# Two-layer network behind clustered attention, one core: the first pair of heads ranks raw centroid products, and the other preparation moves by an iteration

## The chip, the cores and the metric

The program runs on one core of one Trainium2 chip. The metric is device time in microseconds (us), the median of repeated executions of the whole program; lower is better. Engines are named as the profile names them: PE is TensorE (PEld its weight loads), DVE is VectorE, ACT is ScalarE, POOL is GpSimd and SP is SyncE, which here only issues DMA transfers.

## What is computed

Attention within clusters, then two feed-forward layers. The first pair of heads, which the change is about, goes through the cluster assignment like every other.

```python
def _attn_ref(q, k, v, centroids):            # batch 2, heads 8, seq 768, head_dim 64, 16 clusters
    q_n = q / (np.linalg.norm(q, axis=-1, keepdims=True) + 1e-06)
    k_n = k / (np.linalg.norm(k, axis=-1, keepdims=True) + 1e-06)
    c_n = centroids / (np.linalg.norm(centroids, axis=-1, keepdims=True) + 1e-06)
    q_assign = np.argmax(np.einsum('bhsd,hcd->bhsc', q_n, c_n), axis=-1)
    k_assign = np.argmax(np.einsum('bhsd,hcd->bhsc', k_n, c_n), axis=-1)
    mask = q_assign[:, :, :, None] == k_assign[:, :, None, :]
    scores = np.where(mask, scale * np.matmul(q, k.transpose(0, 1, 3, 2)), -1000000000.0)
    ... softmax(scores) @ v

x = attn_out                                   # 1536 tokens x 512
x = leaky_relu(x @ w_in) @ w_out               # d_ff 2048
h = x @ moe2_w_in
out = (P(h) / (Q(h) + 1e-06)) @ moe2_w_out     # cubic over quadratic in |h|
```

## The kernel before

The 16 heads are worked in eight pairs. A head has six query tiles of 128 rows, so a pair is twelve units and the attention 96. A hand-written loop `run` goes over iterations i. Iteration i takes the row maximum of unit i on VectorE (`nm`, L592), divides two units by their sums on GpSimd when i is even (`e`, L619, of units i-2 and i-1), transposes the probabilities of unit i-4 on TensorE (`pT`, L627), takes the exponential of unit i on ScalarE (`e`, L603), and forms the scores of unit i+1 on TensorE (`s`, L583, first with `a`, then with `b`). The transposed probabilities are split in a rounded part `ph` (ScalarE, L640) and a rest `pl` (VectorE, L646), and multiplied with the values `vs`.

Each pair p has to be prepared before its units come up. The rows of q and k are loaded (`qraw`, `kraw`), transposed (`pa`, L243), copied by ScalarE (`x`, L246), and multiplied with the centroids on TensorE (`sims`, L326); the products are copied to `sv` (L337). VectorE then takes the maximum over the 16 clusters (`mx`), marks where it is reached, numbers the marks (`rank`, L362), takes the first (L365) and compares again for the one-hot rows (`oh`). These go through TensorE, ScalarE (`ot`, L429) and six DMA transfers (L436) into the lower rows of `b`, where they mask the scores. The high and low parts of q and k (`hl`, L293 and L298 on GpSimd) go to `a` and `b` by DMA (L305: four transfers for `a`, two for `b` per head). The values `v` of a pair are loaded into one buffer, `vraw` (L233), and split by GpSimd, once per head of the pair (`vsplit`, L447 and L448).

Which iteration does which piece is a table for each pair: an entry (-9, "end", rank) of pair p puts it at the end of iteration 12p-9; "act", "pe", "pa" and "dve" are places earlier in the iteration. Each engine works through its own instructions in the order in which the program issues them, and waits for what it needs; SyncE's transfers stand in one queue in the same way. All GpSimd work and all `vsplit` calls are thus in one order with the divisions `e`.

Pair 0 and the first head of pair 1 are prepared in `startup`, written out by hand ahead of the loop. There the centroids are normalised first, by twelve small VectorE operations (L116 to L129), then transposed into `cc`, and only then multiplied. The first head's one-hot rows go into `b` without DMA (`on`, L387; `po`, L401; L409 and L411), its `a` and `b` parts too (`direct_hi` on ScalarE, `direct_lo` on VectorE L281, `direct_b` on GpSimd L286). The multiplications `warm` (L722) on constant data compute nothing that is used; they keep TensorE occupied.

Of the kernel before, what the change touches and what calls it, by code (L numbers as in the profile page):

```python
# [9 lines left out]
F32 = mybir.dt.float32  # L10
# [8 lines left out]
P = 128  # L19
# [11 lines left out]
def clustered_attention_moe_moe2(  # L31
# [81 lines left out]
    def exact_norm_ops(y, r, ss):  # L113
        vec = nc.vector
        return [
            lambda: vec.tensor_scalar(  # L116
                y.bitcast(I32), ss.bitcast(I32), 0.5, SQRT_MAGIC, op0=ALU.mult, op1=ALU.add
            ),
            lambda: vec.reciprocal(r, y),
            lambda: vec.tensor_tensor(r, r, ss, op=ALU.mult),  # L120
            lambda: vec.tensor_tensor(y, y, r, op=ALU.add),
            lambda: vec.reciprocal(r, y),
            lambda: vec.scalar_tensor_tensor(r, r, 2.0, ss, op0=ALU.mult, op1=ALU.mult),
            lambda: vec.scalar_tensor_tensor(y, y, 0.5, r, op0=ALU.mult, op1=ALU.add),
            lambda: vec.reciprocal(r, y),
            lambda: vec.scalar_tensor_tensor(r, r, 2.0, ss, op0=ALU.mult, op1=ALU.mult),
            lambda: vec.scalar_tensor_tensor(y, y, 0.5, r, op0=ALU.mult, op1=ALU.add),
            lambda: vec.tensor_scalar(y, y, 0.5, 1e-6, op0=ALU.mult, op1=ALU.add),
            lambda: vec.reciprocal(r, y),  # L129
        ]  # L130
# [11 lines left out]
    class Attention:  # L142
# [27 lines left out]
        def load_centroids(self):  # L170
            self.tok.tile([P, 104], F32, name="fill", bufs=1)
            self.ct = self.tok.tile([P, D], F32, name="ct", bufs=1)
            nc.scalar.dma_start(out=self.ct, in_=cent.rearrange("h c d -> (h c) d"))
            nc.scalar.preload_act_table_set("natural_log_exp_and_others")

        def centroid_ops(self):
            sm = self.tok
            ct = self.ct
            sq = sm.tile([P, D], F32, name="csq", bufs=1)
            ss = sm.tile([P, 1], F32, name="css", bufs=1)  # L180
            y = sm.tile([P, 1], F32, name="cy", bufs=1)
            r = sm.tile([P, 1], F32, name="cr", bufs=1)
            ch = sm.tile([P, 2, D], F32, name="ch", bufs=1)
            self.ch = ch
            vec = nc.vector
            ops = [
                lambda: vec.tensor_tensor(sq, ct, ct, op=ALU.mult),
                lambda: vec.reduce_sum(ss, sq, axis=AX.X),
            ]
            ops += exact_norm_ops(y, r, ss)  # L190
            return ops + [
                lambda a=a: vec.tensor_scalar(ch[:, a], ct, r, None, op0=ALU.mult)
                for a in range(2)
            ]
# [1135 lines left out]
```

## Time and profile before

| | before |
|---|---|
| median of 3 runs | 791.07 us (790.88 to 791.53) |
| the profiled execution | 791.8 us |
| span of its records, first to last instruction | 789.7 us |
| TensorE busy | 776.2 us, 98% |
| VectorE, ScalarE, GpSimd busy | 645.8, 510.6, 387.9 us |
| mean granted TensorE clock | 0.997 of 2.4 GHz |
| attention: until about | 262 us |
| feed-forward layers | from 262 us on |

The span is what the trace shows; the profiled execution took 2.1 us more than it. A busy share is an average over the whole program. What a stage is worth is read from the stretch in question: which engine has no idle time there, and what the others wait for. Times in the rows below count from the first instruction.

### The profile page before, as it was taken

The numbers are of one execution on the slowest core, as the hardware profiler recorded it, in microseconds if no ns is written. First come the engines' busy times: TensorE is split into PE (matmuls) and PEld (weight loads), VectorE is DVE, ScalarE is ACT, GpSimd is POOL, SyncE is SP. The second block draws the span as 40 slices with busy tenths as digits, with TensorE's granted clock in tenths as the row PEclk, the third lists the DMA queues.
The fourth block names the chain that finished last, engine by engine and source line by source line (L and its number), as shares of the span: only waits on it lengthen the run. The fifth ranks groups of instructions, "written<-read, shape, count | busy, mean of one in ns | idle before, by whom it ended". The sixth has DMA issues, their size and how long they took to land.

```text
span 789.7 us, 11946 instructions
## 1 busy us (share of the span) xinstructions
PE 776.2 (98%) x4026; PEld 660.1 (84%) x4026; DVE 645.8 (82%) x1106; ACT 510.6 (65%) x1015; POOL 387.9 (49%) x400
## 2 busy tenths in 40 slices
PE   8899999999998999999999999999999999999997
PEld 6699999899887888888888888888888888888886
DVE  7888999998998678877577568759988888888896
ACT  5789998998899455454254246357766666666662
POOL 3876987877567324230041023267645545553341
PEclk9999999999999999999999999999999999999999
DMA  3686663662320334345445353530101001000012
GB/s 103 158 210 140 154 150 83 150 159 78 93 91 1 107 107 161 106 142 205 134 156 181 128 175 114 180 106 30 52 13 41 27 27 41 15 0 1 1 54 107
DMA packets 42109, 78.58 MB, mean 100 GB/s; under 512 B 5248, under 2 KB 25280, under 8 KB 42048
## 3 DMA queue, kind: packets, MB, share of 16 engines
q1 hardware_dynamic: 41760, 77.65, 33.3%
q8 instruction: 32, 0.52, 0.3%
q14 instruction: 29, 0.24, 0.1%
q10 hardware_dynamic: 288, 0.16, 0.1%
HBM read 49.84 MB, written 9.96 MB: 76 GB/s over the span
## 4 chain that ended last, share of the span: by engine, by line
PE 87%; DVE 6%; ACT 3%; POOL 1%; issue 1%; DMA 0%; DVEq 0%; ACTq 0%; POOLq 0%
PE h L1097 33%; PE y L1097 31%; PE o L663 7%; PE s L583 6%; PE pT L627 6%; PE sims L326 3%; DVE pl L646 2%; DVE nm L592 2%; PE pa L243 1%; ACT ph L640 1%; ACT e L603 1%; POOL e L619 1%; PE warm L722 1%; DVE acc L1218 1%; DMA ct<-in_centroids_dram 0%
## 5 line engine op out<-in xcount | busy, mean ns | idle before, releaser
L646 DVE TENSOR_TENSOR pl<-pT,ph 128x384 fp32r<-128x384 f32 x192 | 97.0, 545 | 13.8 <-ACT ph L640 13.6
L619 POOL TENSOR_SCALAR e<-e,sum 128x768 f32<-128x768 f32 x96 | 87.5, 923 | 41.3 <-DVE sum L615 27.4
L920 POOL TENSOR_TENSOR wil<-wf,wih 128x512 fp32r<-128x512 f32 x32 | 42.8, 1350 | 126.4 <-ACT wih L917 114.7
L1130 ACT CAST gh<-h 128x512 fp32r<-128x512 f32 x96 | 56.4, 588 | 69.3 <-DVE h L1177 67.8
L1097 PE MATMUL h<-xha,wil 128*128 128x512 f32 x256 | 99.7, 389 | 0.0
L1097 PE MATMUL h<-xla,wih 128*128 128x512 f32 x256 | 99.7, 389 | 0.0
L1097 PE MATMUL h<-xha,wih 128*128 128x512 f32 x256 | 99.6, 389 | 0.0
L1150 POOL TENSOR_SCALAR z<-y,abv 128x512 f32<-128x512 f32 x48 | 37.0, 771 | 117.3 <-ACT y L1146 117.3
L1135 DVE TENSOR_TENSOR gl<-h,gh 128x512 fp32r<-128x512 f32 x96 | 65.4, 684 | 34.8 <-ACT gh L1130 34.5
L640 ACT CAST ph<-pT 128x384 fp32r<-128x384 f32 x192 | 82.3, 481 | 14.9 <-PE pT L627 13.2
L592 DVE TENSOR_REDUCE nm<-s 128x1 f32<-128x768 f32 x96 | 90.8, 946 | 0.5
L603 ACT ACTIVATE e<-s,nm 128x768 f32<-128x768 f32 x96 | 87.4, 911 | 5.6 <-DVE nm L592 3.0
L627 PE MATMUL pT<-ident,e 128*128 128x128 f32 x576 | 80.7, 275 | 1.5 <-DVE pl L646 1.4
L1218 DVE TENSOR_TENSOR acc<-y,acc 128x512 f32<-128x512 f32 x84 | 56.6, 689 | 29.5 <-PE y L1097 29.2
L910 DVE SCALAR_TENSOR_TENSOR wf<-st,wf 128x512 int32<-128x512 int32 x124 | 80.3, 700 | 0.0
L1097 PE MATMUL y<-gl,woh 128*128 128x512 f32 x192 | 74.8, 390 | 0.0
L1097 PE MATMUL y<-gh,wol 128*128 128x512 f32 x192 | 74.8, 389 | 0.0
L1097 PE MATMUL y<-gh,woh 128*128 128x512 f32 x192 | 74.7, 389 | 0.0
L1097 PE MATMUL y<-woh,gl 128*128 128x512 f32 x191 | 74.4, 390 | 0.0
L1097 PE MATMUL y<-woh,gh 128*128 128x512 f32 x191 | 74.4, 389 | 0.0
L1097 PE MATMUL y<-wol,gh 128*128 128x512 f32 x191 | 74.3, 389 | 0.0
L627 PEld LDWEIGHTS pT<-ident,e 128*128 128x128 f32 x576 | 66.9, 142 | 6.9 <-DVE pl L646 1.6
(130 smaller groups left out, 1905.3 us busy)
## 6 DMA issues: line engine op xcount, KB each, us to landing
st<-in_moe_w_out_dram SPq DMA_DIRECT2D x32, 512.0 KB, 4.4
st<-in_moe_w_in_dram SPq DMA_DIRECT2D x30, 512.0 KB, 4.6
a<-hl SPq DMA_DIRECT2D x56, 192.0 KB, 4.9
b<-hl SPq DMA_DIRECT2D x28, 192.0 KB, 5.7
wf<-scratch_wi SPq DMA_DIRECT2D x14, 256.0 KB, 2.9
qraw<-in_q_dram SPq DMA_DIRECT2D x16, 192.0 KB, 3.5
kraw<-in_k_dram SPq DMA_DIRECT2D x16, 192.0 KB, 3.7
vraw<-in_v_dram SPq DMA_DIRECT2D x8, 384.0 KB, 5.2
```

Of the source, the lines that this page charges most:

```text
L592: nc.vector.reduce_max(un["nm"], un["s"][:, 0:S], axis=AX.X, negate=True)
L603: nc.scalar.activation(un["e"], un["s"][:, 0:S], AF.Exp, bias=un["nm"], accum_out=un["recip"])
L619: nc.gpsimd.tensor_scalar(un["e"], un["e"], un["recip"], 1.0, op0=ALU.mult, op1=ALU.mult)
L627: nc.tensor.transpose(pp[:, kt * P:(kt + 1) * P], un["e"][:, k0:k0 + P], ident)
L640: nc.scalar.copy(un["hi", part], un["pT", part])
L646: nc.vector.tensor_tensor(self.group[gi]["pl"][:, part * n:(part + 1) * n, i * P:(i + 1) * P], un["pT", part], f32(un["hi", part]), op=ALU ...
L663: nc.tensor.matmul(gr["o"], lhsT=self.pair[p]["vs"][:, h * T + tile_of(kt), :], rhs=gr["pl" if j else "ph"][:, kt, :], start=n == 0, stop= ...
L910: nc.vector.scalar_tensor_tensor(wi, hold["st", i][:, :, :, 1 - w], sc, wi, op0=op, op1=ALU.bitwise_or)
L1097: nc.tensor.matmul(o, lhsT=l, rhs=r, start=(first and idx == 0), stop=(last and idx == n - 1),)
L1130: nc.scalar.copy(d["gh"], d["h"])
L1135: nc.vector.tensor_tensor(d["gl"], d["h"], f32(d["gh"]), op=ALU.subtract)
L1218: nc.vector.tensor_tensor(a, y, a, op=ALU.add)
```

## The change

The first head's products no longer wait for the norms. In `startup` the centroids as loaded are transposed and copied (`centroid_raw`), and the products of pair 0 are taken with these; the norms come to the products afterwards, as a row `rr` that VectorE multiplies in (`norm_row`, `sims_scaled`). The norm has nine VectorE operations instead of twelve, and its sum of squares is ScalarE's. The normalised centroids `cc` are built later, from GpSimd's `ch`, for the pairs from 1 on. The keys' one-hot rows come before the queries', and ScalarE writes both into `b`.

The second head's maximum, marks and numbering move into iteration 0, the numbering to GpSimd. The rounded parts of q and k of that head go into `b` by DMA (`place_hi`, 192 KB each) instead of by GpSimd. Pair 1's preparation moves by one to two iterations, and so does most of pair 2's; the values of pair 1 are loaded in iteration 8 instead of 6, as the last piece there, and the second `vsplit` of pair 0 is in iteration 7 instead of 4. `warm` calls: 20 ahead of the loop instead of 24, and four each in iterations 0, 2 and 3 instead of five in 0 to 3. Whatever follows pair 2 is as before.

```diff
+            for a in range(2):
+                nc.scalar.dma_start(out=self.ct[:, a], in_=cent.rearrange("h c d -> (h c) d"))
...
+            nc.scalar.activation(self.csq, self.ct[:, 0], AF.Square, scale=0.25, accum_out=ss)
+            exact_norm_ops(y, r, ss, s4, s16)
+            nc.vector.tensor_scalar(self.diag, ident[:, 0:HP * C], r, None, op0=ALU.mult)
+            nc.gpsimd.tensor_scalar(self.ch, self.ct, r, 1.0, op0=ALU.mult, op1=ALU.mult)
+
+        def centroid_raw(self, tile_, first):
+            pp = tile_("pcr")[:, 0:P]
+            nc.tensor.transpose(pp, self.ct.rearrange("p a d -> p (a d)"), ident)
+            first()
+            for a in range(2):
+                r = slice(a * D, (a + 1) * D)
+                nc.scalar.copy(
+                    self.cr[r, :, a], pp[r, 0:HP * C].rearrange("p (h c) -> p h c", h=HP)
+                )
+
+        def norm_row(self, tile_):
+            pp = tile_("prr")[:, 0:HP * C]
+            nc.tensor.matmul(pp, lhsT=self.ones, rhs=self.diag, start=True, stop=True)
+            nc.vector.tensor_copy(self.rr, pp)
...
                 r = slice(a * D, (a + 1) * D)
-                nc.vector.tensor_copy(
+                nc.scalar.copy(
                     cc[r, :, a], pp[r].rearrange("p (h c) -> p h c", h=H)
                 )
...
+
+            def place_hi(h, i):
+                nc.sync.dma_start(
+                    out=f32(st["b"][0:D, i, h]), in_=f32(st["a"][h][i * D:(i + 1) * D, i])
...
                     st["pp"].pop(("s", h))[:, 0:NS2 * C].rearrange("p (n c) -> p n c", c=C),
+                )
+
+            def sims_scaled(h):
+                if h == 0:
+                    st["sv"] = tok.tile([P, HP, NS2, C], F32, tag="sv", name="sv")
+                rr = self.rr[:, h * C:(h + 1) * C].unsqueeze(1).to_broadcast([P, NS2, C])
+                nc.vector.tensor_tensor(
+                    st["sv"][:, h],
+                    st["pp"].pop(("s", h))[:, 0:NS2 * C].rearrange("p (n c) -> p n c", c=C),
+                    rr, op=ALU.mult,
...
             if p == 0:
                 plan = [
-                    (0, "act", direct_hi, 1, 0),
+                    (0, "pe", f1_x_out, 0),
+                    (1, "pe", direct_hi, 1, 0),
+                    (1, "end", place_hi, 1, 0),
                     (1, "end", onehot_t, (1, 2)),
+                    (2, "pe", direct_hi, 1, 1),
                     (2, "act", onehot_out, (1, 2)),
-                    (2, "act", direct_hi, 1, 1),
                     (2, "dve", direct_lo, 1, 0),
-                    (2, "end", direct_b, 1, 0),
+                    (2, "end", place_hi, 1, 1),
                     (2, "end", place_oh, (1, 2)),
                     (3, "dve", direct_lo, 1, 1),
-                    (3, "end", direct_b, 1, 1),
-                    (4, "end", vsplit, 1),
+                    (7, "end", vsplit, 1),
                 ]
             if p == 1:
                 early = [
-                    (-12, "pa", sims, 0),
-                    (-11, "act", sims_out, 0),
-                    (-11, "pa", trans, 1, 0),
-                    (-11, "pa", trans, 1, 1),
+                    (-13, "pe", trans, 0, 0),
+                    (-13, "pe", trans, 0, 1),
+                    (-11, "pa", sims, 0),
                     (-11, "end", split_hi, 0),
-                    (-11, "end", split_lo, 0, 0),
-                    (-11, "end", split_lo, 0, 1),
-                    (-10, "act", trans_out, 1, 0),
-                    (-10, "act", trans_out, 1, 1),
-                    (-10, "pa", sims, 1),
-                    (-9, "act", sims_out, 1),
-                    (-9, "dve", sims_max),
-                    (-9, "dve", is_max),
-                    (-9, "end", rank),
-                    (-9, "end", split_hi, 1),
-                    (-9, "end", split_lo, 1, 0),
-                    (-9, "end", place_a, 0),
-                    (-9, "end", place_b, 0),
-                    (-8, "dve", first),
-                    (-8, "dve", onehot, 0),
-                    (-8, "dve", onehot, 1),
-                    (-8, "end", split_lo, 1, 1),
-                    (-7, "pe", onehot_t),
-                    (-7, "end", place_a, 1),
-                    (-7, "end", place_b, 1),
-                    (-6, "act", onehot_out),
-                    (-6, "end", place_oh),
+                    (-10, "act", sims_out, 0),
+                    (-10, "end", split_lo, 0, 0),
+                    (-9, "pa", trans, 1, 0),
+                    (-9, "pa", trans, 1, 1),
+                    (-9, "end", split_lo, 0, 1),
+                    (-8, "act", trans_out, 1, 0),
+                    (-8, "act", trans_out, 1, 1),
+                    (-8, "pa", sims, 1),
+                    (-8, "end", place_a, 0),
+                    (-8, "end", place_b, 0),
+                    (-7, "act", sims_out, 1),
+                    (-7, "dve", sims_max),
+                    (-7, "dve", is_max),
+                    (-7, "end", rank),
+                    (-7, "end", split_hi, 1),
+                    (-7, "end", split_lo, 1, 0),
+                    (-6, "dve", first),
+                    (-6, "dve", onehot, 0),
+                    (-6, "dve", onehot, 1),
+                    (-6, "end", split_lo, 1, 1),
+                    (-5, "pe", onehot_t),
+                    (-4, "act", onehot_out),
+                    (-4, "end", place_oh),
+                    (-4, "end", place_a, 1),
+                    (-4, "end", place_b, 1),
+                    (-4, "end", load_v),
                 ]
...
-            for f in self.centroid_ops():
-                f()
-            warm(8)
+            self.centroid_norms()
+            warm(7)
             halves(f0, 0)
-            warm(3)
-            self.centroid_t(pq)
+            self.centroid_raw(pq, lambda: f0["x_out"](0, (0,)))
+            f0["x_out"](0, (1,))
+            warm(6)
+            f0["sims"](0, pq, self.cr, 0, 1)
+            f0["direct_hi"](0, 0, (0,))
+            f0["direct_lo"](0, 0, (0,))
+            f0["direct_b"](0, 0, (0,))
+            self.norm_row(pq)
+            f0["sims"](0, pq, self.cr, 1, 2)
             halves(f0, 1)
-            warm(2)
+            load_consts()
             f1["load_qk"]()
             f0["load_v"]()
-            f0["x_out"](0)
-            f0["sims"](0, pq)
-            f0["direct_hi"](0, 0)
-            f0["direct_lo"](0, 0)
-            f0["direct_b"](0, 0)
+            f0["direct_hi"](0, 1)
+            f0["direct_b"](0, 1)
             f0["x_out"](1)
-            f0["sims_out"](0)
+            f0["direct_hi"](0, 0, (1,))
+            f0["direct_b"](0, 0, (1,))
+            f0["sims_scaled"](0)
             f0["sims_max"](h0)
             f0["is_max"](h0)
             f0["rank"](h0, vec)
             f0["first"](h0)
+            f0["onehot_near"](1, 0)
             f0["onehot_near"](0, 0)
-            f0["onehot_near"](1, 0)
-            f0["direct_hi"](0, 1)
+            warm(3)
+            f0["sims"](1, pq, self.cr)
+            near = {i: self.ring("po") for i in (1, 0)}
+            for i in (1, 0):
+                f0["onehot_near_t"](i, near[i])
+            f0["onehot_near_out"](1, 0)
+            f0["onehot_near_out"](0, 0, (0,))
+            f0["onehot_near_out"](0, 0, (1,))
             f0["direct_lo"](0, 1)
-            f0["direct_b"](0, 1)
-            f0["sims"](1, pq)
-            f0["sims_out"](1)
-            warm(9)
-            near = [self.ring("po") for i in range(2)]
-            for i in range(2):
-                f0["onehot_near_t"](i, near[i])
-            f0["onehot_near_out"](0, 0)
-            f0["onehot_near_out"](1, 0)
-            f0["sims_max"](h1)
-            f0["is_max"](h1)
-            for i in range(2):
-                f1["trans"](0, i)
-            f1["x_out"](0)
-            warm(2)
+            f0["direct_lo"](0, 0, (1,))
+            self.centroid_t(pq)
+            warm(4)
             f0["vsplit"](0)
...
+                if i == 0:
+                    f0 = self.pair[0]["fn"]
+                    f0["sims_scaled"](1)
+                    f0["sims_max"]((1, 2))
+                    f0["is_max"]((1, 2))
+                    f0["rank"]((1, 2))
                 if i == 1:
-                    f0 = self.pair[0]["fn"]
-                    f0["rank"]((1, 2), nc.vector)
                     f0["first"]((1, 2))
                     f0["onehot"](0, (1, 2))
                     f0["onehot"](1, (1, 2))
...
-                if 0 <= i < TL:
-                    self.warm(5)
+                if i in (0, 2, 3):
+                    self.warm(4)
```

In the table of pair 2 most entries go one iteration later, for example `(-22, "end", load_qk)` to `(-21, "end", load_qk)`.

SyncE's queue, where pair 1 is placed (L305 the parts of q and k, L436 the one-hot rows, L233 the values of pair 1), before:

```order
L305 DMA a<-hl 64x2x384 x4
L305 DMA b<-hl 64x2x384 x2
L305 DMA a<-hl 64x2x384 x4
L305 DMA b<-hl 64x2x384 x2
L436 DMA b<-ot 16x4x128 x6
L233 DMA vraw<-in_v_dram 128x2x384
L226 DMA qraw<-in_q_dram 128x384
```

and now (L323 the parts, L466 the one-hot rows, L246 the values):

```order
L323 DMA a<-hl 64x2x384 x4
L323 DMA b<-hl 64x2x384 x2
L466 DMA b<-ot 16x4x128 x6
L323 DMA a<-hl 64x2x384 x4
L323 DMA b<-hl 64x2x384 x2
L246 DMA vraw<-in_v_dram 128x2x384
L239 DMA qraw<-in_q_dram 128x384
```

The one-hot rows of pair 1 now stand ahead of its second head's six transfers, and the load of the values behind all twelve.

GpSimd at the first `vsplit` of pair 1 (L447 and L448; L298 the low part of pair 2's heads, L619 the divisions, L362 the numbering for pair 2), before:

```order
L447 TENSOR_SCALAR vs<-vraw 128x6x64
L448 TENSOR_TENSOR vs<-vraw,vs 128x6x64
L298 TENSOR_TENSOR hl<-x,hl 128x384 x2
L619 TENSOR_SCALAR e<-e,sum 128x768 x2
L447 TENSOR_SCALAR vs<-vraw 128x6x64
L448 TENSOR_TENSOR vs<-vraw,vs 128x6x64
L362 TENSOR_TENSOR sv<-sv,iom 128x384
L619 TENSOR_SCALAR e<-e,sum 128x768 x2
```

and now (L477 and L478, L311 and L316 the parts, L653, L391):

```order
L477 TENSOR_SCALAR vs<-vraw 128x6x64
L478 TENSOR_TENSOR vs<-vraw,vs 128x6x64
L311 TENSOR_SCALAR hl<-x 128x2x384
L316 TENSOR_TENSOR hl<-x,hl 128x384
L653 TENSOR_SCALAR e<-e,sum 128x768 x2
L477 TENSOR_SCALAR vs<-vraw 128x6x64
L478 TENSOR_TENSOR vs<-vraw,vs 128x6x64
L316 TENSOR_TENSOR hl<-x,hl 128x384
L391 TENSOR_TENSOR sv<-sv,iom 128x384
L653 TENSOR_SCALAR e<-e,sum 128x768 x2
```

Between the first `vsplit` and the divisions stood two low parts; now the copy and the low part of one array stand there, and the other low part of pair 2's second head follows the second `vsplit`, ahead of the numbering. In both orders the numbering for pair 2 and the divisions of units 12 and 13 (the last row) come behind.

VectorE from the second half of the first head to the second head's one-hot rows, before (L592 row maximum, L362 numbering):

```order
L281 TENSOR_TENSOR a<-x,a 64x384 x2
L411 CAST b<-po 16x768
L354 TENSOR_REDUCE mx<-sv 128x12
L357 TENSOR_TENSOR sv<-sv,mx 128x192
L592 TENSOR_REDUCE nm<-s 128x1 x2
L362 TENSOR_TENSOR sv<-sv,iom 128x192
L365 TENSOR_REDUCE mx<-sv 128x12
L372 TENSOR_TENSOR oh<-iom,mx 128x96 x2
L592 TENSOR_REDUCE nm<-s 128x1
```

and now (L626 row maximum, L394 takes the first of the numbered marks):

```order
L293 TENSOR_TENSOR a<-x,a 64x384 x3
L626 TENSOR_REDUCE nm<-s 128x1
L365 TENSOR_TENSOR sv<-sims,c_142 128x192
L383 TENSOR_REDUCE mx<-sv 128x12
L386 TENSOR_TENSOR sv<-sv,mx 128x192
L626 TENSOR_REDUCE nm<-s 128x1
L394 TENSOR_REDUCE mx<-sv 128x12
L401 TENSOR_TENSOR oh<-iom,mx 128x96 x2
L626 TENSOR_REDUCE nm<-s 128x1
```

The numbering between L386 and L394 is gone from VectorE, and the product with the norms (L365) is new.

## Rows read from the trace of the kernel before

**Rows 1.** Stretches: length, busy time of each engine, granted clock, DMA share, GB/s.

```profile
52.00:66.00 14.00, 14.00 (x100) 13.15 (x99) 13.83 (x28) 13.52 (x33) 8.53 (x10) 1.00 1.08 225
...
21.00:22.00 1.00, 0.10 (x1) 0.00 (x0) 1.00 (x1) 0.97 (x3) 1.00 (x2) 1.00 0.04 11
...
24.00:25.00 1.00, 1.00 (x5) 0.71 (x3) 0.90 (x2) 0.97 (x3) 0.74 (x1) 0.50 0.07 16
```

**Rows 2.** The timeline, first 17 us: start, length, engine, line, work.

```profile
1.32 2.74 PE L722 MATMUL warm<-warm_in 128*128 128x384 bf16 x8 [1.32 <-DVE warm_in L72]
...
5.38 0.87 ACT L246 ACTIVATE x<-pa 128x384 f32<-128x384 f32 x2 [2.92 <-PE pa L243]
...
7.98 2.79 PE L326 MATMUL sims<-cc,x 128*128 128x32 f32 x24
...
12.16 1.22 DVE L281 TENSOR_TENSOR a<-x,a 64x384 fp32r<-64x384 f32 x2
...
12.68 0.80 ACT L409 ACTIVATE b<-po 16x768 fp32r<-16x768 f32 x1 [1.48 <-PE po L401]
...
14.34 0.51 POOL L447 TENSOR_SCALAR vs<-vraw 128x384 fp32r<-128x384 f32 x1 [2.49 <-DMA vraw<-in_v_dram]
...
14.51 0.59 PE L583 MATMUL s<-b 80*128 80x512 f32 x2
...
15.17 1.82 DVE L592 TENSOR_REDUCE nm<-s 128x1 f32<-128x768 f32 x2
```

**Rows 3.** The timeline from 18 to 25 us, VectorE.

```profile
18.13 0.35 DVE L365 TENSOR_REDUCE mx<-sv 128x12 f32<-128x192 f32 x1
...
23.09 2.06 DVE L281 TENSOR_TENSOR a<-x,a 64x384 fp32r<-64x384 f32 x2
```

**Rows 4.** The timeline, iterations 6 and 8, ScalarE and VectorE.

```profile
33.67 0.66 ACT L429 ACTIVATE ot<-po 96x256 fp32r<-96x256 f32 x2
...
36.74 0.94 DVE L592 TENSOR_REDUCE nm<-s 128x1 f32<-128x768 f32 x1
...
37.68 0.86 ACT L640 CAST ph<-pT 128x384 fp32r<-128x384 f32 x2
```

**Rows 5.** The timeline, SyncE's queue, 34 to 44 us.

```profile
34.00 2.54 SPq L305 DMA_DIRECT2D a<-hl  x4
...
37.96 4.68 SPq L436 DMA_DIRECT2D b<-ot  x6
...
42.69 0.58 SPq L233 DMA_DIRECT2D vraw<-in_v_dram  x1
43.38 0.41 SPq L226 DMA_DIRECT2D qraw<-in_q_dram  x1
```

**Rows 6.** The timeline, GpSimd, 46 to 55 us.

```profile
46.26 0.51 POOL L447 TENSOR_SCALAR vs<-vraw 128x384 fp32r<-128x384 f32 x1 [0.74 <-DMA vraw<-in_v_dram]
...
47.81 1.97 POOL L298 TENSOR_TENSOR hl<-x,hl 128x384 fp32r<-128x384 f32 x2
49.76 1.79 POOL L619 TENSOR_SCALAR e<-e,sum 128x768 f32<-128x768 f32 x2
...
53.78 1.01 POOL L362 TENSOR_TENSOR sv<-sv,iom 128x384 f32<-128x384 f32 x1 [0.64 <-DVE sv L357]
```

**Rows 7.** The timeline, 51 to 59 us, VectorE, ScalarE, then TensorE.

```profile
51.30 0.94 DVE L592 TENSOR_REDUCE nm<-s 128x1 f32<-128x768 f32 x1
52.17 1.00 DVE L646 TENSOR_TENSOR pl<-pT,ph 128x384 fp32r<-128x384 f32 x2
...
55.45 0.54 DVE L365 TENSOR_REDUCE mx<-sv 128x24 f32<-128x384 f32 x1
...
57.58 0.90 ACT L603 ACTIVATE e<-s,nm 128x768 f32<-128x768 f32 x1
...
58.62 0.61 PE L583 MATMUL s<-a 128*128 128x512 f32 x2
```

**Rows 8.** Tile vraw (loads of 384 KB): issue to landing.

```profile
DMA to landing us min/median/max: 2.9/5.2/10.6
```

More of the change, by code (lines that the diff above doesn't have):

```diff
@@ L111, in x1_slices, with exact_norm_ops, newton @@
                 yield nm, slice(b - lo, e - lo), slice(b - t0, e - t0)
-    def exact_norm_ops(y, r, ss):
+    def exact_norm_ops(y, r, ss, s4, s16):
         vec = nc.vector
[L115 to L130, printed above, removed]
+        def newton(sc):
+            vec.reciprocal(r, y)
+            vec.scalar_tensor_tensor(y, r, sc, y, op0=ALU.mult, op1=ALU.add)
+        vec.tensor_scalar(
+            y.bitcast(I32), ss.bitcast(I32), 0.5, SQRT_MAGIC, op0=ALU.mult, op1=ALU.add
+        )
+        for sc, k in ((s4, 4.0), (s16, 16.0)):
+            nc.gpsimd.tensor_scalar(sc, ss, k, 1.0, op0=ALU.mult, op1=ALU.mult)
+        for sc in (ss, s4, s16):
+            newton(sc)
+        vec.tensor_scalar(y, y, 0.5, 1e-6, op0=ALU.mult, op1=ALU.add)
+        vec.reciprocal(r, y)
     xf_t = {}
@@ L170, in load_centroids @@
         def load_centroids(self):
-            self.tok.tile([P, 104], F32, name="fill", bufs=1)
-            self.ct = self.tok.tile([P, D], F32, name="ct", bufs=1)
-            nc.scalar.dma_start(out=self.ct, in_=cent.rearrange("h c d -> (h c) d"))
+            c0 = self.tok.tile([P, 4, BLK], F32, tag="hl", name="c0", bufs=2)
+            self.ct = c0[:, 0, 0:2 * D].rearrange("p (a d) -> p a d", a=2)
+            self.ones = c0[:, 1, 0:P]
+            self.diag = c0[:, 2, 0:HP * C]
+            self.rr = c0[:, 2, 64:64 + HP * C]
@@ L174, in load_centroids, with centroid_norms @@
+            self.csq = c0[:, 3, 0:D]
+            self.cr = c0[:, 3, P:P + HP * 2 * C].rearrange("p (h u c) -> p h u c", h=HP, u=2)
+            for a in range(2):
+                nc.scalar.dma_start(out=self.ct[:, a], in_=cent.rearrange("h c d -> (h c) d"))
             nc.scalar.preload_act_table_set("natural_log_exp_and_others")
-        def centroid_ops(self):
+        def centroid_norms(self):
             sm = self.tok
[L178 to L194, printed above, removed]
+            ss, s4, s16, y, r = (
+                sm.tile([P, 1], F32, name=nm, bufs=1) for nm in ("css", "cs4", "cs16", "cy", "cr")
+            )
+            sm.tile([P, 8], F32, name="fill", bufs=1)
+            self.ch = sm.tile([P, 2, D], F32, name="ch", bufs=1)
+            nc.scalar.activation(self.csq, self.ct[:, 0], AF.Square, scale=0.25, accum_out=ss)
+            exact_norm_ops(y, r, ss, s4, s16)
+            nc.vector.tensor_scalar(self.diag, ident[:, 0:HP * C], r, None, op0=ALU.mult)
+            nc.gpsimd.tensor_scalar(self.ch, self.ct, r, 1.0, op0=ALU.mult, op1=ALU.mult)
@@ L257, in part, with x_out, direct_parts @@
                 return st["hl"][h][:, 3 * i + 2 * s * (1 - 2 * i)]
-            def x_out(h):
-                st["x"][h] = tok.tile([P, 2, W], F32, tag="x", name="x", bufs=3)
-                for i in range(2):
-                    scaled_copy(st["x"][h][:, i], i, st["pp"].pop(("a", h, i)))
-            def direct_parts(h, i):
-                for u in range(2):
+            def x_out(h, parts=(0, 1)):
+                for i in parts:
+                    trans_out(h, i)
+            def direct_parts(h, i, us=(0, 1)):
+                for u in us:
                     yield st["x"][h][u * D:(u + 1) * D, i], *(
@@ L318, in place_b, with sims @@
                 move(st["b"][0:D, :, h], h, slice(0, 4, 3), queues)
-            def sims(h, tile_=self.ptile):
-                pp = tile_("sims")
-                st["pp"]["s", h] = pp
+            def sims(h, tile_=self.ptile, rhs=cc[:, g * HP:(g + 1) * HP], i0=0, i1=2):
+                if i0 == 0:
+                    st["pp"]["s", h] = tile_("sims")
+                pp = st["pp"]["s", h]
                 w = 2 * C
-                for j in range(T):
+                for j in range(i0 * TH, i1 * TH):
                     i, t = divmod(j, TH)
@@ L394, in onehot_near, with f1_x_out @@
                 )
+            def f1_x_out(h):
+                self.pair[1]["fn"]["x_out"](h)
             def onehot_near_t(i, pp):
```

74 lines of the change are left out of this document (38 added, 36 removed).

## The prediction

> **What bounds the kernel now.** I read the stretches first. From 52 to 66 us TensorE is busy for 14.00 of 14.00 us and VectorE for 13.83 [rows 1]: in the steady attention TensorE has no idle time, so what the start gains or loses is carried to the end one for one, unless a later wait eats it. The feed-forward layers follow from attention and keep their own order. The change can therefore act only in the first 60 us, and I follow two moments through it: the row maximum of unit 8 (before at 36.74 [rows 4]) and the scores of unit 17 on TensorE (before at 58.62 [rows 7]). Behind the second the order of work is the same as before but for small shifts in pair 2.
>
> **The head start.** Before, the products of both heads of pair 0 run from 7.98 for 2.79 us [rows 2], so the first head's end at 9.4. They wait for the norms and for `cc`. Now they need the raw copies and `x`. Seven `warm` instead of eight, at 2.74 / 8 = 0.34 us each, bring `x` from 5.38 to 5.1; it takes 0.44 us a half [rows 2], two small copies of the raw centroids stand between the halves (0.25 each, my estimate from the 0.32 to 0.35 us that three times as wide operations take [rows 3]), so `x` is complete at 6.5. TensorE comes out of its six new `warm` at about 6.9 and needs 2.79 / 2 = 1.4 us: 8.3, plus the norms' row, 8.4, 1.0 us earlier. Bounds: 9.4 (nothing gained) and 7.9 (no wait behind `warm`).
>
> From there five VectorE steps at 0.35 and a gap of some 0.04 [rows 3] and one one-hot half (0.37) end at 10.75; the transposes of the keys take 0.7 with their way out, ScalarE's copy 0.80 [rows 2], the queries' first half about half of that. So the masked half of the first scores starts at 12.8 instead of 14.51, and with the same 0.66 from there the first row maximum at **13.5 instead of 15.17** [rows 2]. The VectorE copy of the keys' rows and three of the norm's operations cost nothing more: ScalarE has idle time there (1.48 us ahead of its copy [rows 2]).
>
> **VectorE from unit 0 to unit 8.** It is the engine the others wait for in iterations 0 to 8, so I add up its queue as the new order has it:
> - eight row maxima at 52.17 - 51.30 = 0.87 [rows 7]: 7.0
> - four pairs of `pl` at 1.00 [rows 7]: 4.0
> - pair 1's maximum, marks and first at 0.54 [rows 7], and its one-hot rows at 0.8 (two more of the same kind, shorter): 2.4
> - the second head's product, maximum, marks and first at 0.39 [rows 3], and its one-hot rows 0.75: 2.3
> - its four `direct_lo` at 1.22 / 2 = 0.61 [rows 2]: 2.4
>
> Sum 18.1 us. To it come three waits that the new order makes. First, the numbering on GpSimd stands behind `vsplit` of head 0, and that waits for `vraw` (before until 14.34 [rows 2]). The load stands behind transposes that end 1.0 later, so I put it at 15.3; `vsplit` takes 47.81 - 46.26 = 1.55 [rows 6], the numbering half of 1.01 [rows 6]: 17.4. VectorE would be ready at 13.5 + 2 x 0.87 + 3 x 0.39 = 16.4: 1.0 lost, and the row maximum of unit 2 queues behind it. Second, pair 1's second head is now transposed in iteration 3 and holds two of three PSUM buffers until ScalarE has copied it behind `ph`; the second half of unit 0's `pT` then waits for the first half's `ph` and `pl`: 0.9 (0.43 + 0.5 [rows 4, 7]). Third, the products of that head (2.79 / 2 = 1.4 [rows 2]) stand ahead of unit 1's `pT` in iteration 4 or 5: 1.2. Together 3.1, between 0 (all hidden) and 4.5. Unit 8 is reached at 13.5 + 18.1 + 3.1 = 34.7, **2.0 us earlier** than 36.74. So of the work that pair 1 gives up in iterations 0 to 3, most comes back in 4 to 7, where VectorE has no room.
>
> One row speaks for less: a pair of `direct_lo` took 2.06 us at 23.09 [rows 3] where it takes 1.22 at 12.16 [rows 2]. GpSimd was copying `b` in that time, and the low parts of `hl` stand there now. The Trainium skill (SBUF — State Buffer, SBUF: two separate sides) says that a VectorE operation with two SBUF inputs and a GpSimd operation that reads SBUF take one port pair in turn, each for its whole length. By that rule one pair would be slowed again and unit 8 come at 35.5, and the sum below be 0.8 more; by the row without neighbours it is as above, which I keep.
>
> **The values of pair 1.** This is the term that decides. GpSimd's `vsplit` of pair 1 stands in iteration 10 as before, ahead of the divisions of units 10 to 13 and of the numbering for pair 2. Before, `vraw` was issued at 42.69, behind six transfers of one-hot rows, and GpSimd waited 0.74 us for it until 46.26 [rows 5, 6]. The twelve transfers ahead of it had begun at 34.00, so twelve take 8.7 us of SyncE's queue [rows 5]. Now the one-hot rows come first, in iteration 8, and the same twelve begin only when ScalarE has written `ot`: `ph` of unit 4 moves with unit 8's row maximum from 37.68 to 35.7, takes 0.86, `ot` 0.66 [rows 4]: 37.2. The load is issued at 37.2 + 8.7 = 45.9. It landed in 3.6 us before (42.69 to 46.26), behind small one-hot transfers [rows 5]; the loads of `vraw` span 2.9 to 10.6 us with a median of 5.2 [rows 8], and this one follows six transfers of `a` and `b`, 192 KB each. I take 4.5, between the row and the median: **50.4 instead of 46.26**.
>
> The Trainium skill (DMA: Bandwidth & Descriptors, Anatomy of one DMA) fits a transfer as 2.0 us and its bytes over 436 GB/s, which for 393 kB would be an estimate of 2.9 us and bring the sum down by 1.6. That fit is measured on another issuing path, and the row of 3.6 already disagrees.
>
> What is behind it on GpSimd, up to the numbering for pair 2: `vsplit` 1.55, `hl` 0.9 (a copy, priced as one division) and 1.0, two divisions 1.8, `vsplit` 1.55, `hl` 1.0, numbering 1.0 [rows 6], 8.8 us, to 59.2 (before 54.8). VectorE stands at `first` for it and takes 0.54; the row maximum of unit 15 queues behind that, 0.87, then the exponential, 0.90, which frees the buffer for the scores of unit 17 [rows 7]: with gaps 61.6 instead of 58.62. On the way the divisions of units 10 to 13 are late by as much, and TensorE's `pT` of these units with them, so no other engine can pass.
>
> **Sum.** 61.6 - 58.6 = +3.0: the head start of 2.0 less, 5.0 of waiting for the values more. The profiled execution took 791.8, its span 789.7; +3.0 gives 794.8. The median of the runs lies 0.7 below that execution, so **794.1 us**. At nothing I cost three edits. The twelve `warm` fewer stood where TensorE waits for ScalarE or VectorE; if that cover is gone, the third rival below is the price. `place_hi` puts two transfers ahead of the second head's one-hot rows; unit 6 needs these in iteration 5, where the wait for `pT` of unit 1 hides them, otherwise up to 1 us. Pair 2's pieces, one iteration later, have twelve iterations to their first unit, apart from the numbering that is in the sum.
>
> **Rivals.** 0.2% is 1.6 us, about what runs of this kernel can tell from no change.
> - *The values come in time.* The place is SyncE's queue. A load of q took 0.41 us there [rows 5]; at that and a small gap the twelve would take 5.4, the load would go out at 42.6 and land, in 2.9 to 3.6, at 45.5 to 46.2: 789.2 to 789.9. It decides at a landing of 47.4; earlier than that the kernel is not slower. Against it stand the queue's own twelve, 0.72 each, which the order of the queue shows behind no data.
> - *A head start of 5.* If all three waits of VectorE are hidden, unit 8 comes at 31.6, the load goes out at 42.8 and lands at 47.3: the two cancel, 791. For it: ScalarE and TensorE have idle time to fill; against it: VectorE's queue is in order, and it was busy for 13.83 of 14.00 us later on [rows 1].
> - *The clock falls as well.* TensorE was busy for 0.10 of the microsecond from 21 us, and at 24 us the granted clock was 0.50, 1.2 GHz [rows 1]. Waits of 1 to 3 us between 54 and 61 us could bring that again, where before nothing was lost; some 3.5 us at half would cost 1.7: 795.8.
> - *No head start*, because `warm` and the transposes ahead of the products hold TensorE: 1.7 more, 795.8 too.
>
> **Chances.** Forecast 0.41, clock or no head start 0.14, a head start of 5 0.22, values in time 0.23, of which 0.20 below 789.5. So faster by over 0.2%: 0.20; within: 0.25; slower: 0.55. The forecast's own range is 792.5 (three waits half hidden, landing in 3.6) to 796.5 (landing in 7). The whole range of 789.0 to 797.0 leaves out two tails of about 0.1 each: values in time and a large head start together, and a landing near the longest row with a lower clock.
>
> **What would show it.** On GpSimd in the changed profile, an idle time of several us ahead of the first `vs` near 45 to 50 us, put down to the load of `vraw`; on TensorE waits for `e` or for the exponential between 52 and 61 us; the first row maximum near 13.5 and a short wait of VectorE for GpSimd's numbering near 17. If the wait ahead of `vs` is under 2 us, the sum is wrong in its main term; if unit 8's row maximum comes before 33 us, the three waits are.

## The result, and the profile after

The changed kernel takes **798.2 us** (median of six runs, 796.4 to 799.15) against 791.65 for the kernel before: 1.0079 times as long, with a 95% interval of 1.0068 to 1.009. Slower was forecast, but by 2.5 to 3.0 us; it is 6.5, and 798.2 lies above the range. The profiled execution has a span of 796.6 (before 789.7).

The timeline of the changed kernel, in order of time; the time in brackets is idle time of the engine just before, and what ended it.

```profile
13.62 0.96 DVE L626 TENSOR_REDUCE nm<-s 128x1 f32<-128x768 f32 x1 [0.62 <-PE s L617]
...
17.96 0.35 DVE L394 TENSOR_REDUCE mx<-sv 128x12 f32<-128x192 f32 x1 [1.35 <-POOL sv L391]
...
19.97 1.73 DVE L293 TENSOR_TENSOR a<-x,a 64x384 fp32r<-64x384 f32 x2
...
22.44 2.27 POOL L316 TENSOR_TENSOR hl<-x,hl 128x384 fp32r<-128x384 f32 x2
...
22.72 2.41 DVE L293 TENSOR_TENSOR a<-x,a 64x384 fp32r<-64x384 f32 x2
...
24.36 0.49 PE L661 MATMUL pT<-ident,e 128*128 128x128 f32 x3
...
26.11 0.54 DVE L680 TENSOR_TENSOR pl<-pT,ph 128x384 fp32r<-128x384 f32 x1
...
26.70 0.55 PE L661 MATMUL pT<-ident,e 128*128 128x128 f32 x3 [1.84 <-DVE pl L680]
...
27.66 0.88 ACT L259 ACTIVATE x<-pa 128x384 f32<-128x384 f32 x2
...
27.80 0.56 DVE L680 TENSOR_TENSOR pl<-pT,ph 128x384 fp32r<-128x384 f32 x1 [1.15 <-ACT ph L674]
...
28.21 1.53 PE L345 MATMUL sims<-cc,x 128*128 128x32 f32 x12 [0.26 <-ACT x L259]
...
29.57 0.85 PE L661 MATMUL pT<-ident,e 128*128 128x128 f32 x6
...
30.64 1.02 DVE L680 TENSOR_TENSOR pl<-pT,ph 128x384 fp32r<-128x384 f32 x2 [1.42 <-ACT ph L674]
...
37.97 0.94 DVE L626 TENSOR_REDUCE nm<-s 128x1 f32<-128x768 f32 x1
...
39.16 0.66 ACT L459 ACTIVATE ot<-po 96x256 fp32r<-96x256 f32 x2
...
39.84 3.85 SPq L466 DMA_DIRECT2D b<-ot  x6
...
43.79 3.44 SPq L323 DMA_DIRECT2D a<-hl  x4
...
47.28 1.42 SPq L323 DMA_DIRECT2D b<-hl  x2
...
48.80 0.55 SPq L246 DMA_DIRECT2D vraw<-in_v_dram  x1
...
52.88 0.94 DVE L626 TENSOR_REDUCE nm<-s 128x1 f32<-128x768 f32 x1
...
53.10 0.51 POOL L477 TENSOR_SCALAR vs<-vraw 128x384 fp32r<-128x384 f32 x1 [6.34 <-DMA vraw<-in_v_dram]
53.68 0.52 PE L256 MATMUL pa<-ident,qraw 128*128 128x128 f32 x3 [1.57 <-DMA qraw<-in_q_dram]
...
61.16 1.01 POOL L391 TENSOR_TENSOR sv<-sv,iom 128x384 f32<-128x384 f32 x1
...
62.20 0.55 DVE L394 TENSOR_REDUCE mx<-sv 128x24 f32<-128x384 f32 x1 [2.26 <-POOL sv L391]
...
65.16 0.99 PE L617 MATMUL s<-a 128*128 128x512 f32 x2
```

The two moments that the prediction followed: the row maximum of unit 8 stands at 37.97, against 36.74 in [rows 4], and the scores of unit 17 at 65.16, against 58.62 in [rows 7]: 6.5 us late, the whole loss. Between them the row maximum of unit 13 is at 52.88, against 51.30 in [rows 7]: 1.6 late. So 1.6 of the loss is there before the values of pair 1 are missed, and 5.0 come after. The rows of ScalarE, SyncE and GpSimd from 39.16 on give the chain of those 5.0: `ot`, twelve transfers, the load at 48.80, its landing and the split at 53.10, the numbering at 61.16.

Stretches of the changed kernel (length, busy time of each engine, granted clock, DMA share, GB/s); the first answers to [rows 1].

```profile
52.00:66.00 14.00, 9.46 (x61) 8.41 (x61) 9.45 (x16) 9.09 (x23) 12.38 (x14) 0.95 1.08 269
20.00:22.00 2.00, 2.00 (x8) 1.12 (x8) 1.94 (x3) 1.93 (x5) 1.96 (x2) 0.55 0.44 98
...
26.00:28.00 2.00, 1.25 (x7) 0.89 (x7) 0.82 (x3) 0.72 (x2) 1.71 (x2) 1.00 0.20 37
...
66.00:68.00 2.00, 2.00 (x8) 1.81 (x8) 1.97 (x6) 1.30 (x4) 1.50 (x2) 0.50 1.08 201
```

TensorE is busy for 9.46 us where it was busy for 14.00: 4.5 us of idle time in this one stretch, where there was none.

### The profile page after: what moved, and what is told of

Its sections match the earlier page's. It is cut to its first block, busy times and chain, and to the rows that moved or that the text cites. A ratio compares the mean times of both kernels' runs of the same rounds, so it can differ in the third digit from the quotient of the medians.

```text
span 796.6 us, 11939 instructions
## 1 busy us (share of the span) xinstructions
PE 777.7 (98%) x4017; PEld 660.3 (83%) x4017; DVE 645.1 (81%) x1100; ACT 511.5 (64%) x1021; POOL 387.9 (49%) x404
## 4 chain that ended last, share of the span: by engine, by line
PE 83%; DVE 8%; ACT 3%; DMA 2%; POOL 2%; issue 1%; SPq 1%; DVEq 0%; POOLq 0%; ACTq 0%
PE h L1134 31%; PE y L1134 31%; PE o L697 6%; PE pT L661 5%; PE s L617 5%; PE sims L345 2%; DVE pl L680 2%; DVE nm L626 2%; ACT ph L674 1%; PE pa L256 1%; ACT e L637 1%; DMA a<-hl 1%; POOL e L653 1%; DVE acc L1255 1%; DMA vraw<-in_v_dram 1%
## 5 line engine op out<-in xcount | busy, mean ns | idle before, releaser
L653 POOL TENSOR_SCALAR e<-e,sum 128x768 f32<-128x768 f32 x96 | 87.8, 926 | 42.2 <-DVE sum L649 31.9
L674 ACT CAST ph<-pT 128x384 fp32r<-128x384 f32 x192 | 82.3, 480 | 20.4 <-PE pT L661 18.8
L626 DVE TENSOR_REDUCE nm<-s 128x1 f32<-128x768 f32 x96 | 90.8, 946 | 1.1 <-PE s L617 0.6
```

What stands on the lines that cost most here:

```text
L626: nc.vector.reduce_max(un["nm"], un["s"][:, 0:S], axis=AX.X, negate=True)
L653: nc.gpsimd.tensor_scalar(un["e"], un["e"], un["recip"], 1.0, op0=ALU.mult, op1=ALU.mult)
L674: nc.scalar.copy(un["hi", part], un["pT", part])
```

## The experiments

Times are medians; behind them the ratio to the kernel before on the same chip, with its 95% interval. The kernel before had 791.6 to 792.0 in all of these.

### Between unit 0 and unit 8

**The copies out of PSUM first.** ScalarE empties the two buffers that pair 1's second head holds ahead of unit 0's `ph`, not behind it:

```diff
-(-8, "act", trans_out, 1, 0), (-8, "act", trans_out, 1, 1),
+(-8, "dve0", trans_out, 1, 0), (-8, "dve0", trans_out, 1, 1),
```

> The changed kernel; ScalarE copies the transposes of pair 1's second head out of PSUM before the first ph instead of behind it, so that two of three buffers come free before unit 0's second pT half. Theory (that buffer wait, 1.84 us on TensorE, and what queues behind it cost the head start): second pT half within 0.5 us of the first, 796.5 to 797.5. Rival (VectorE's queue is short of time in iterations 4 to 7 whatever TensorE does): 798.

**794.15 us, 1.003 (1.0017 to 1.0044)**: 4 us less, more than expected. Its timeline:

```profile
17.20 0.35 DVE L394 TENSOR_REDUCE mx<-sv 128x12 f32<-128x192 f32 x1 [1.16 <-POOL sv L391]
...
23.18 0.85 ACT L259 ACTIVATE x<-pa 128x384 f32<-128x384 f32 x2
23.46 0.82 PE L661 MATMUL pT<-ident,e 128*128 128x128 f32 x6
...
24.82 1.42 PE L345 MATMUL sims<-cc,x 128*128 128x32 f32 x12
...
26.07 0.88 PE L661 MATMUL pT<-ident,e 128*128 128x128 f32 x6
...
34.48 0.94 DVE L626 TENSOR_REDUCE nm<-s 128x1 f32<-128x768 f32 x1
...
49.40 0.94 DVE L626 TENSOR_REDUCE nm<-s 128x1 f32<-128x768 f32 x1
...
63.78 0.95 DVE L626 TENSOR_REDUCE nm<-s 128x1 f32<-128x768 f32 x1
```

All six transposes of unit 0 now stand in one row. In the changed kernel 5.2 us pass from unit 0's first `pT` to unit 1's (24.36 to 29.57), here 2.6. Unit 8 stands at 34.48; the prediction said 34.7. The first row maximum of this execution is at 13.04, 0.6 earlier than in the changed kernel's (the kernels with one and the same start show 12.50 to 13.87 there), so 2.9 of the 3.5 us at unit 8 are the edit's. The 1.16 at 17.20 is the only wait of VectorE over 0.1 us between unit 0 and unit 8; the changed kernel has three, 1.35, 1.15 and 1.42. Over all profiled executions that stretch takes 21.0 to 21.6 us in the five kernels with these copies and the new tables, and 24.2 to 25.7 in the six without them.

**The numbering on VectorE.**

```diff
-f0["rank"]((1, 2))
+f0["rank"]((1, 2), nc.vector)
```

> The changed kernel with the second head's numbering on VectorE instead of GpSimd. Theory (VectorE's wait of 1.35 us at 17.96 is filled again before unit 8 by waits for PSUM and for the products of pair 1): 797.5 to 798.5. Rival (that wait is carried to unit 8): 796.5 to 797.

798.89 us, 1.0086 (1.0057 to 1.0115): no gain. It does not show that VectorE's wait at 17.96 is free: the numbering itself takes 1.07 us on VectorE (at 15.90), so little of the 1.35 could come back.

**TensorE kept busy in iteration 1.**

```diff
-if i in (0, 2, 3):
+if 0 <= i < TL:
     self.warm(4)
```

> The changed kernel with four warm products in iteration 1 too. Theory (the granted clock of 0.55 to 0.60 from 20 to 24 us follows TensorE's idle time at 18 to 19, and costs 1 to 1.5 us there): clock 1.00 from 20 to 24, 796.5 to 797.5. Rival (VectorE, slowed beside GpSimd, sets the pace there, not TensorE): 798, or more where warm products stand in the way.

797.51 us, 1.0077 (1.0062 to 1.0092): as the changed kernel. Its stretches:

```profile
20.00:22.00 2.00, 2.00 (x15) 1.55 (x14) 1.94 (x3) 1.50 (x5) 2.00 (x3) 1.00 0.44 98
...
24.00:26.00 2.00, 0.10 (x1) 0.10 (x2) 1.81 (x4) 0.00 (x0) 0.51 (x1) 1.00 0.10 26
...
28.00:30.00 2.00, 2.00 (x12) 2.00 (x11) 0.51 (x1) 0.61 (x2) 0.00 (x0) 0.50 0.85 273
```

The clock is full from 20 to 22, where it was 0.55, but TensorE still stands for 1.9 of 2 us from 24. So the low clock is not the cause of that wait. It comes behind it instead, at 0.50 from 28 to 32, so the unchanged time does not say what the half clock costs.

### The values of pair 1

**The split later.** The load stays; GpSimd splits in iterations 12 and 14 and divides first:

```diff
 (-4, "end", load_v),
+(0, "end", vsplit, 0), (2, "end", vsplit, 1),
```

> The load stays where the changed kernel has it; only GpSimd's split of pair 1 moves back, from iterations 10 and 12 to 12 and 14, so that GpSimd divides units 10 to 13 first. Theory: the divisions are no longer late, 793 to 794, and what is left above the kernel before the split early would give is TensorE's wait for the q load of pair 3 (1.57 us). Rival (queue): 796.5 to 798, with TensorE waiting for transfers.

795.16 us, 1.0037 (1.0019 to 1.0054): 3 us back, not 4 to 5, between the two expectations. GpSimd now stands elsewhere, in its timeline at 52.14:

```profile
52.14 0.83 POOL L311 TENSOR_SCALAR hl<-x 128x768 fp32r<-128x768 f32 x1 [4.93 <-DMA b<-hl]
```

This is pair 2's `hl`. There are two such buffers, and the late transfers of pair 1 still read one.

**The load earlier**, first line; the second is pair 0's split, which frees the buffer of `vraw`:

```diff
-(-4, "end", load_v),
+(-5, "end", load_v),
-(7, "end", vsplit, 1),
+(4, "end", vsplit, 1),
```

> Pair 1's load of vraw goes one iteration earlier, ahead of the twelve transfers of its rows; the second half of pair 0's split, which frees its buffer, goes back to iteration 4. Theory (about 5 of the 6.5 us lost come from the wait of GpSimd for that load, the other 1.5 from preparation that fills iterations 5 and 6): no wait over 1 us ahead of the split of pair 1, 793 us. Rival (the twelve transfers themselves, or SyncE's queue behind them, hold the first scores of pair 1 and the transposes of pair 3; the split only happens to wait meanwhile): 796.5 to 798.

797.64 us, 1.0064 (1.0042 to 1.0086): only 0.6 less, a miss. The wait for `vraw` is gone, but GpSimd waits 4.32 us ahead of the same `hl`, at 52.51; part of the rest is the clock (0.50 from 30 to 34 us in this execution).

**The load and the second head's six transfers earlier.** To the last edit comes:

```diff
-(-4, "end", place_a, 1), (-4, "end", place_b, 1),
+(-5, "end", place_a, 1), (-5, "end", place_b, 1),
```

> The kernel of the early load, and the six transfers of pair 1's second head too stand one iteration earlier, ahead of the one-hot rows. Theory (the late transfers hold GpSimd twice: first through vraw, and where that is gone through the buffer of hl, for which it waited 4.32 us at 52.51 in the early-load run): no wait of GpSimd over 1.5 us between 46 and 56, its numbering for pair 2 near 56 instead of 59.0, 793 to 794. Rival (what is left in the early-load run is the half clock from 28 to 35 us, not GpSimd): 796.5 to 797.5.

799.25 us, 1.0099 (1.0074 to 1.0123): a miss to the other side. The wait only changes its place: GpSimd still waits 2.52 us for `vraw`, at 48.19, and the one-hot rows, now last, hold the first scores of pair 1 (the granted clock is 0.66 from 48 to 58 us as well):

```profile
49.04 0.59 PE L617 MATMUL s<-b 80*128 80x512 f32 x2 [1.83 <-DMA b<-ot]
```

**The one-hot rows on ScalarE's queue**, with the early copies:

```diff
-(-4, "end", place_oh),
+(-4, "end", place_oh, ALL, (nc.scalar,)),
```

> The early copies out of PSUM, and pair 1's six transfers of one-hot rows are issued on ScalarE's queue instead of SyncE's. Theory (what is left, 2.5 us, is the twelve transfers in one queue): load of vraw out near 41 instead of 45, GpSimd's wait ahead of the split under 2 us instead of 6.08, 790.5 to 792. Rival (ScalarE pays for the issues, 0.6 us each, with ph and the exponentials behind them): vraw early but 794 to 796.

794.26 us, 1.0032 (1.0019 to 1.0045), the rival's case. The load goes out at 41.95 and GpSimd does not wait for it, but ScalarE's timeline shows what the issues cost there:

```profile
37.17 3.67 ACTq L466 DMA_DIRECT2D b<-ot  x5
40.88 0.86 ACT L674 CAST ph<-pT 128x384 fp32r<-128x384 f32 x2 [3.67 <-DMA b<-ot]
...
54.09 0.94 DVE L626 TENSOR_REDUCE nm<-s 128x1 f32<-128x768 f32 x1
...
63.56 0.94 DVE L626 TENSOR_REDUCE nm<-s 128x1 f32<-128x768 f32 x1
```

The last two rows are units 13 and 17. They are 9.5 us apart, as in the kernel before, where the early copies alone have 14.4: with the values in time, this stretch loses nothing. But unit 13 itself is 4.7 later than with the early copies alone, so the run does not show what an early load is worth without ScalarE's price.

**Early copies and later split together.**

> Two edits on the changed kernel: the early copies out of PSUM (alone 4.0 us) and the later split of pair 1 (alone 3.0 us). Theory (two separate losses, one in iterations 4 to 6, one in iterations 10 to 15): they add, 791 us, within 0.7. Rival (both edits recover the same time): 793.5 to 794.2.

792.3 us, 1.0011 (0.9998 to 1.0024): 5.9 of 7.0. The interval reaches the rival's 793.5, but the traces show two separate losses. Time between row maxima in the profiled executions, us:

| kernel | unit 0 to 8 | 8 to 13 | 13 to 17 | 17 to 24 |
|---|---|---|---|---|
| before | 21.6 | 14.6 | 9.5 | 18.1 |
| changed | 24.4 | 14.9 | 14.7 | 18.8 |
| copies first | 21.4 | 14.9 | 14.4 | 17.6 |
| split later | 25.5 | 14.9 | 11.7 | 17.6 |
| both | 21.5 | 14.9 | 12.0 | 19.3 |

The copies shorten only the first stretch, the later split only the third, and with both some of it is lost again behind unit 17. GpSimd waits 5.28 us ahead of `hl` and TensorE 1.11 for pair 3's q. Two more runs moved GpSimd's work away from that wait, the first with the upper two lines, the second with all four:

```diff
-(-14, "end", split_hi, 1), (-13, "end", split_lo, 1, 0), (-12, "end", split_lo, 1, 1),
+(-12, "end", split_hi, 1), (-12, "end", split_lo, 1, 0), (-11, "end", split_lo, 1, 1),
-(0, "end", vsplit, 0), (2, "end", vsplit, 1),
+(2, "end", vsplit, 0), (3, "end", vsplit, 1),
```

> The two edits that together gave 792.3 us, and GpSimd's high and low parts of pair 2's second head moved behind the divisions of units 10 and 11. Theory (what is left is GpSimd standing 5.28 us ahead of hl at 48.99, whose buffer the late transfers of pair 1 still read, with these divisions queued behind it): the numbering for pair 2 near 54 instead of 55.48, 790.5 to 791.3. Rival (the rest is TensorE's wait for the q load, 1.11 us, or the order of work itself): 792 to 792.6.

> The same, and pair 1's split another two iterations later, behind the numbering for pair 2. Theory: the numbering near 52.5 to 53.5, VectorE's wait for it (1.56 us) gone, 789.8 to 790.6. Rival: 792 to 792.6.

792.15 us, 1.0 (0.999 to 1.0009), and 791.95 us, 1.0001 (0.9991 to 1.001): no gain, the rival's numbers. In the first the numbering came at 55.75, not near 54. In the second it came at 52.56, VectorE no longer waits for the numbering, and the time is lost further on, in its timeline:

```profile
49.54 0.52 PE L256 MATMUL pa<-ident,qraw 128*128 128x128 f32 x3 [1.24 <-DMA qraw<-in_q_dram]
...
62.72 0.88 PE L663 MATMUL pT<-ident,e 128*128 128x128 f32 x6 [1.20 <-POOL e L655]
...
68.14 0.83 POOL L311 TENSOR_SCALAR hl<-x 128x768 fp32r<-128x768 f32 x1 [3.61 <-DMA a<-hl]
```

TensorE waits for q, then for GpSimd's divisions, and GpSimd for pair 3's `hl`. That last wait is no loss by itself: the kernel before has one of 3.76 us there (at 66.36) and the fastest kernel below 3.10, and in neither does TensorE wait for a division behind it.

### The start by itself

**New start, old tables.** All iterations of pairs 1 and 2 are those of the kernel before, except for the first two transposes of pair 1, which the new start leaves to iteration -1; some of the lines:

```diff
-(-7, "dve", sims_max),
+(-9, "dve", sims_max),
...
-(-4, "end", place_oh),
+(-6, "end", place_oh),
...
-(-21, "end", load_qk),
+(-22, "end", load_qk),
...
-(7, "end", vsplit, 1),
+(4, "end", vsplit, 1),
```

> New start (raw centroid products, keys' rows first, second head's ranking on GpSimd), but the preparation of pairs 1 and 2 in the iterations of the kernel before. Theory (the start is worth 1.5 us and keeps it; the moved preparation eats it between units 5 and 8): 789.5 to 790.5, unit 8's row maximum at 35. Rival (the start gives its 1.5 us back by itself, through the numbering on GpSimd behind the split): 791.5, unit 8's row maximum at 36.5 or later.

792.87 us, 1.0007 (0.999 to 1.0023): no gain, a miss for the theory, and not for the rival's reason. The timeline:

```profile
23.53 3.92 SPq L466 DMA_DIRECT2D b<-ot  x6
27.55 0.53 SPq L239 DMA_DIRECT2D qraw<-in_q_dram  x1
...
30.20 0.88 PE L256 MATMUL pa<-ident,qraw 128*128 128x128 f32 x3 [3.10 <-DMA qraw<-in_q_dram]
...
30.87 1.49 PE L660 MATMUL pT<-ident,e 128*128 128x128 f32 x6
```

Pair 2's loads stand behind `place_hi`, which waits for ScalarE, and the one-hot rows. TensorE waits 3.10 us, and then runs at a granted clock of 0.50 from 30 to 34: six transposes take 1.49 where they take 0.82.

**The same, pair 2's loads of q and k first.**

```diff
-(-22, "end", load_qk),
+(-22, "pa", load_qk),
```

> The kernel of the old tables, with pair 2's loads of q and k put ahead of the copies of hi and the one-hot rows in SyncE's queue, in the same iteration. Theory (the start gives its gain back because these loads went out at 27.55 instead of 24.49: TensorE waited 3.10 us for qraw and then ran from 30 to 36 at a granted clock of 0.50): no such wait, clock 1.00 from 28 on, unit 8's row maximum near 35, 789 to 790. Rival (another wait takes its place, since the one-hot rows now go out later): 792 to 793.

**789.51 us, 0.998 (0.9967 to 0.9993)**: faster than both kernels. Unit 8 stands at 33.99, the loads go out at 20.39, and the clock is 1.00 in every stretch from 18 to 80 us.

**The kernel before, loads first** (that one line alone):

> The kernel before, with only pair 2's loads of q and k put ahead of the one-hot rows in SyncE's queue. Theory (the 2 us that the best kernel gains on it are the new start's; in the kernel before nothing waits for these loads): 791.2 to 792. Rival (the gain is that of the earlier loads): 789.5.

791.92 us, 1.0003 (0.9987 to 1.0018): nothing. The 2.1 us are the start's, with all that it brings along; its parts were not run one by one.

**The best, split later** (the two `vsplit` entries at 0 and 2):

> The new start with the old tables and the early loads of q and k (789.5 us), and pair 1's split two iterations later as well. Theory (with the values in time GpSimd waits only 0.64 us for them, and that is hidden): 789.2 to 789.8, no change. Rival (GpSimd has no slack there either): 788.5 to 789.

**789.19 us, 0.997 (0.9958 to 0.9983)**, the fastest of all; against 789.51 that is no difference that these runs tell.

## Why the prediction was right in direction and wrong in size

- **The start: right.** The first row maximum is at 13.62 (said 13.5, before 15.17). With nothing late behind it that is worth 2.1 to 2.7 us (789.51 and 789.19).
- **VectorE from unit 0 to unit 8: wrong, and this is the step that failed.** The sum said 18.1 us of work and 3.1 of waits, 21.2; the stretch took 24.35 (13.62 to 37.97), so unit 8 came 1.2 us late instead of 2.0 early, and everything behind it with it. The three waits were there, each a little longer: 1.35, 1.15 and 1.42, together 3.9. The second and third come as described: unit 0's second `pT` half waits for a PSUM buffer, and behind its `ph` ScalarE copies the transposes, then TensorE takes the products, then unit 1's `pT`. The larger error is in the work, 20.4 us with its small gaps instead of 18.1. Most of it is one term, the low parts: their two pairs took 1.73 and 2.41, together 4.1, where the sum has 2.4. It priced them by the 1.22 of a pair at the start and set the 2.06 of [rows 3] aside. In the kernel before, the other pair of that place was slow too:

```profile
20.35 1.73 DVE L281 TENSOR_TENSOR a<-x,a 64x384 fp32r<-64x384 f32 x2
```

- **What lost the head start** is another question. Against the kernel before, whose low parts were nearly as slow and whose waits in this stretch were 1.14 and 0.49, the waits are the difference; the copies first take the second and third away. That this run's 794.15 meets the forecast's 794.1 is luck: the 2.1 us of waits that the forecast counted for these two are gone there, and 2.2 us of work that it did not count stand in their place.
- **The port rule.** The Trainium skill (SBUF — State Buffer, SBUF: two separate sides) says that the two engines take turns. The rows agree that both are slowed side by side: VectorE's pair at 22.72 took 2.41 where 1.22 stands in [rows 2], GpSimd's `hl` at 22.44 took 2.27 where 1.97 stands in [rows 6]. They do not show turns of whole length: both were done at 25.13, 2.7 us after the first began, and 1.22 and 1.97 one after the other would be 3.2. The prediction let this rule slow one pair, for 0.8 us, and set it aside; it was two pairs and 1.7. No run took the neighbour away, so the cause of the 1.7 is argued and only its size is shown.
- **The values of pair 1: right in each link.** `ot` is written by 39.8, twelve transfers take 9.0 (said 8.7), the load lands in 4.3 (4.5), GpSimd needs 9.1 to the numbering's end (8.8). From unit 13 to unit 17 this cost the 5.0 that were said. What no run shows is the 5.0 as a gain: the later split gave 3.0 back, the earlier load 0.6. I missed that the late transfers hold GpSimd through `hl` too, and TensorE through the q load (1.57). With the split moved, the first of these takes the place of the wait for `vraw`. By the fit of the Trainium skill (DMA: Bandwidth & Descriptors, Anatomy of one DMA) the estimate for the load was 2.9 us, short of the 4.3 measured.
- **`place_hi` at nothing: right here, not in itself.** With pair 2's old table the one-hot rows behind it began at 23.53 instead of 20.47, the loads behind them were as late, and the start's whole gain was gone.
- **The clock: a rival that happened** (0.55 and 0.50), as a consequence of waits, but not free. Of the six executions with the new tables and without the early copies, four ran near 0.50 from 28 to 32 us and took 25.4 to 25.7 us from unit 0 to unit 8; the two at 1.00 took 24.2 and 24.4. In two of the four, VectorE's wait for unit 1's `ph` is 2.91 and 3.00 us instead of 1.42. As their edits differ, 1.2 us for the half clock there is an estimate.

What stays open: with both losses taken out the new tables still give 792, the old ones 789.2 with the same start. The last of the new tables and the fastest kernel, whose profiled executions are 4.5 us apart, are 0.3 apart at unit 13 (49.07 and 48.77), 1.2 at unit 17 (59.73 and 58.54) and 4.6 at unit 24 (80.62 and 76.04): most is lost behind unit 17. The traces show waits at `hl`, q and the divisions that change place with each edit. How the rest divides among them was not settled.

## What to carry to other kernels

When work is moved to a later iteration, follow what its results let go, not only who uses them: here a PSUM buffer, an `hl` buffer and a place in a queue were each held longer, and each wait stood behind another in an in-order queue. Price an operation by the row of the place where it will run, with the neighbours it has there: the low parts took 1.22 us alone and 1.73 to 2.41 beside GpSimd. Look at the loads of the next stage when the start gets faster: here moving one line of loads ahead turned no gain into 2.1 us. And when a time comes out as forecast, check the terms: here one run met the forecast by two errors that cancel.

## What the runs showed of the hardware

An issue of a transfer costs ScalarE's queue about as much as SyncE's: five took 3.67 us, 0.73 each; on SyncE six took 3.85 in the changed kernel and 4.68 in the kernel before, 0.64 and 0.78 each.

In three executions the granted clock stood near 0.50 (1.2 GHz) for some 3 to 7 us behind a wait of TensorE: 1.73 us until 64.23 in the changed kernel, 2.83 until 25.90 with `warm` in iteration 1, 3.10 until 30.20 with the old tables. TensorE was busy for 1.80 to 2.00 of each 2 us there. Not every wait had this: behind 1.84 us until 26.70 in the changed kernel the clock stayed at 1.00.

A pair of GpSimd's operations beside VectorE's low parts is slowed as well: two divisions took 2.43 us at 20.05 instead of 1.79 [rows 6].
